# A long convolution that feeds a grouped mixture of experts: where the side work of rounds two and three stands in their first stages

## The chip, the cores and the metric

The kernel runs on one core of a Trainium2 chip. The metric is the device time of one execution in microseconds (us). Five engines work side by side, each through its own instructions in order: TensorE (PE; its weight loads are shown as PEld), VectorE (DVE), ScalarE (ACT), GpSimd (POOL) and SyncE (SP), which here only issues DMAs.

## What is computed

The reference first convolves, for 8 batches, a sequence of 5056 rows and 128 channels with a filter h, by a Fourier transform of twice the length, a product and the inverse. The 40448 rows that come out then go through 16 experts in 4 groups, each row to the best expert of its best group.

```python
Xf = np.fft.rfft(x, n=2 * S, axis=1);  Hf = np.fft.rfft(h, n=2 * S, axis=0)
x = np.fft.irfft(Xf * Hf[None], n=2 * S, axis=1)[:, :S].reshape(B * S, D)
g_idx = argmax(x @ w_group);  e_idx = argmax(xg @ w_expert[g])
out[tok] = g_w * e_w * (np.maximum(xg @ w1[g, e], 0.0) @ w2[g, e])
```

## The kernel before, in words

**Rounds and stages.** The transform is done in two factors, in three rounds of three slots each: round one (`r = 0`) takes the filter and two batches, rounds two and three (`r = 1`, `r = 2`) three batches each. A round has a first stage (`stage1`), then the groups (`groups`: the second factor, the product with the filter's transform and its inverse), which write to DRAM (`zd`). What is left of a round, its side work (`side`), is done in pieces between the steps of what follows: that of round one during round two, that of round two during round three, that of round three during the experts' blocks.

**The first stage.** It has 48 loads of 160 KB and 96 steps `k`, two for each load. Of every five loads three are folded (small matmuls, line 421, then a copy on ScalarE to `odd`, line 438, and a sum and a difference on VectorE, lines 439 and 440) and two are not (full matmuls, line 427, then one copy on ScalarE, line 444). A load's matmuls go to a pair of PSUM banks `pp`, of which rounds two and three have three. When a load has been evacuated, ScalarE's queue issues the next ones (line 404). The input tiles are named `xt` and `xy`.

**The side work.** It is a list of steps, each with a place `t` on a line of 68.55 slots. Per eighth of a round and 8 slots there are two lumps (lines 721 and 735: the last factor, into the banks `py0` and `py1`, which ScalarE copies to `yT`, line 742), at 0 and 3; the logits matmuls (line 788, read `yT`; copied to `lT`, line 793) with four transposes of rows (line 778), at 4.7; the logits' transpose (line 798) with four more, at 6.4; the remaining row transposes, at 9.5. Some forty small steps of routing on VectorE (`gate_math`) lie between 6.5 and 12.1. Then 10 or 15 scatters stand in a list, of which `send` issues one: a cast on VectorE (line 853) and an indirect DMA on GpSimd (line 854). A lump asks for rows of its successor: `zm` (line 703) behind its first matmuls, four `zt` (line 708), and a second `zm`, all in SyncE's queue.

**The order.** `run` writes one list `main` of steps with weights, and `weave` goes through it. A step of the first stage weighs `W_S1` = 0.45, two steps of each pair of groups 2.0 each, all else nearly always 0. Each weight pays for side steps in proportion, and those are emitted right behind it:

```python
s["acc"] += w / s["len"]
while s["done"] < len(s["steps"]) and (s["sacc"] < s["acc"] * s["total"] - 1e-6 or i == s["end"] - 1):
    sw, sf, small = s["steps"][s["done"]]
    if small and room[i + 1] > 0 and i < s["end"] - 1:
        light.append(sf)
```

A small step is put off and spread over the following steps of weight 0; the others are emitted at once. In rounds two and three `send` stands behind every second step (line 1666 and after). Side work of the round before starts behind step 18 of round two's first stage, and behind step 20 of round three's; that of round one ends behind step 20 of round three's.

Of the kernel before, what the change touches and what calls it, by code (L numbers as in the profile page):

```python
# [47 lines left out]
W_S1, W_END = 0.45, 2.5  # L48
# [182 lines left out]
class Kernel:  # L231
# [1391 lines left out]
    def run(self):  # L1623
        tc = self.tc
        with ExitStack() as ctx:
            self.pools(ctx)
            with ExitStack() as c2:
# [10 lines left out]
                def add(f, w=0.0):  # L1638
                    main.append((w, f))

                def late(r):
                    return [f for p in gr[r][1][NQ // 2:] for _, f in p]

                def advance(g):
                    return lambda: next(g, None)
# [11 lines left out]
                for r in range(3):  # L1657
                    if r == 1:
                        add(self.share)
                    pre, steps = gr[r]  # L1660
                    rest = late(r - 1) if r > 0 else []
                    n = len(s1[r][1])
                    t0 = self.table_0()
                    for k, f in enumerate(s1[r][1]):
                        add(f, W_S1)
                        if r > 0 and k % 2 == 1:
                            add(self.send)
                        if r == 0:
                            add(advance(more))
                        if r == 2 and ("end", 0) in mark:  # L1670
                            add(advance(t0))
                        if k >= 1:
                            for g in rest[RP * k - RP:RP * k]:
                                add(g)
                        if k == SIDE0 and r > 0:
                            add(side[r - 1][0])
                        if k == max(SIDE0 + SIDEG, END0 if r == 2 else 0) and r > 0:
                            mark["start", r - 1] = len(main)
                            if r == 2:
                                mark["end", 0] = len(main)  # L1680
                        if k >= n - PRE and (k - n) % 5 == 0:
                            add(advance(pre))
                    if r > 0:
                        add(lambda: None, W_END)
                    for p in range(0, NQ, 2):
                        for w, f in steps[p // 2]:
                            add(f, w)
                        if p >= NQ - LOAD1:
                            add(advance(s1[r + 1][0] if r < 2 else early))
# [74 lines left out]
```

## Time and profile before

| | us |
|---|---|
| median of three runs | 1758.63 |
| the three runs | 1750.66, 1758.63, 1761.71 |
| the profiled execution | 1759.51 |
| its span, first to last instruction | 1757.7 |

The profile is of one execution on one core. A stage's stretch is given in us from the span's start. Clock figures are TensorE's granted clock as a share of full speed, which is 2.4 GHz; the lower level is 1.2 GHz. "issue" is time in which an engine waited for nothing that the profile shows. TensorE runs a float32 matmul in several passes, so it shows more records than the program has matmuls: 32 for a folded load, 8 for one that is not.

### The profile page before, as it was taken

The page shows a single profiled execution, that of the slowest core. Times are in us where ns is not written, and L with a number is a line of the kernel's source. Part 1 is how long each engine was busy: PE and PEld are TensorE (multiplying, and loading weights), DVE is VectorE, ACT ScalarE, POOL GpSimd, SP SyncE. Part 2 cuts the span into 40 slices and gives each one's busy share as a digit, 9 for nine tenths or more (in the row PEclk, how much of TensorE's full clock was granted, in tenths as well). Part 3 has the DMA queues.
Part 4 walks back from the last instruction along what each step waited for, and adds up shares of the span by engine and source line. Part 5 has one row for each costly group of instructions (what it writes and reads, how often), then busy time and mean ns, then how long its engine had stood idle before and what let it go on. Part 6 is the DMA issues. An engine that isn't in the chain of part 4 may idle for free. (4 is left out here: it accounts for less than half of the span.)

```text
span 1757.7 us, 48202 instructions
## 1 busy us (share of the span) xinstructions
PE 1661.5 (95%) x16765; PEld 1299.0 (74%) x16765; DVE 1297.0 (74%) x3080; ACT 1043.0 (59%) x2461; POOL 769.0 (44%) x742
## 2 busy tenths in 40 slices
PE   8998899988898998999999999999999999999997
PEld 8677756567655556777777778787788877888987
DVE  6554598864586787777777778887787778877876
ACT  5564444443343445666666666676666666666765
POOL 1451243442454454144455545254565554334444
PEclk9999999999998999999999999999999999999999
DMA  7796677876487777555665654447545584444554
GB/s 219 229 299 204 179 249 237 275 230 182 145 247 232 244 226 212 168 165 163 171 175 167 171 152 147 133 144 227 186 148 156 166 254 136 130 129 146 156 164 152
DMA packets 281640, 330.26 MB, mean 188 GB/s; under 512 B 33335, under 2 KB 216000, under 8 KB 281368
## 3 DMA queue, kind: packets, MB, share of 16 engines
q1 hardware_dynamic: 252504, 271.00, 52.2%
q0 software_dynamic: 20608, 41.79, 6.9%
q10 hardware_dynamic: 8256, 14.10, 2.8%
q8 instruction: 140, 2.29, 0.6%
q14 instruction: 132, 1.08, 0.2%
HBM read 230.41 MB, written 96.86 MB: 186 GB/s over the span
## 5 line engine op out<-in xcount | busy, mean ns | idle before, releaser
L854 POOL DMA_INDIRECT srt<-rw,pos x320 | 344.9, 1078 | 450.0 <-DVE pos L853 173.4
L1421 POOL DMA_INDIRECT out<-orow,at x176 | 182.2, 1035 | 254.4 <-ACT at L1419 200.8
L539 DVE TENSOR_TENSOR y<-pp,hg 128x768 f32<-128x768 f32 (+1 forms) x120 | 103.8, 865 | 79.1 <-ACT hg L529 31.1
L1421 POOL DMA_INDIRECT out<-orow,sids x92 | 94.0, 1022 | 116.8 <-DVE orow L1388 83.7
L589 PE MATMUL pp<-y,cg 64*64 64x384 f32 (+1 forms) x1472 | 118.7, 444 | 14.4 <-DVE m L539 10.6
L599 ACT COPY zs<-pp 128x768 f32<-128x768 f32 (+1 forms) x118 | 85.2, 722 | 79.2 <-PE pp L589 40.2
L439 DVE TENSOR_TENSOR st<-pp,odd 128x320 f32<-128x320 f32 x90 | 44.2, 491 | 104.3 <-ACT odd L438 102.4
L521 PE MATMUL pp<-st,cg 64*64 64x192 f32 (+1 forms) x1556 | 117.8, 407 | 0.8 <-issue 0.4
L721 PE MATMUL py<-ig,zm 126*64 126x79 f32 x2048 | 95.5, 243 | 18.7 <-issue 15.1
L721 PEld LDWEIGHTS py<-ig,zm 126*64 126x64 f32 x2048 | 82.1, 142 | 39.2 <-issue 28.0
L1356 DVE SCALAR_TENSOR_TENSOR h0l<-px,h0h 128x512 fp32r<-128x512 f32 (+1 forms) x109 | 73.5, 675 | 50.1 <-ACT h0h L1355 34.9
L742 ACT COPY yT<-py 128x474 f32<-128x474 f32 (+1 forms) x96 | 44.6, 513 | 106.2 <-PE py L735 86.6
L1355 ACT ACTIVATE h0h<-px 128x512 fp32r<-128x512 f32 (+1 forms) x109 | 63.9, 586 | 73.6 <-PE px L1352 47.3
L539 DVE TENSOR_TENSOR m<-pp,hg 128x768 f32<-128x768 f32 (+1 forms) x120 | 102.9, 858 | 1.2 <-ACT hg L531 1.2
L1356 DVE SCALAR_TENSOR_TENSOR h2l<-px,h2h 128x512 fp32r<-128x512 f32 (+1 forms) x112 | 75.5, 674 | 37.8 <-ACT h2h L1355 28.9
L589 PEld LDWEIGHTS pp<-y,cg 64*64 64x64 f32 x1472 | 59.2, 133 | 53.4 <-issue 26.7
L1356 DVE SCALAR_TENSOR_TENSOR h3l<-px,h3h 128x512 fp32r<-128x512 f32 (+1 forms) x111 | 74.6, 672 | 30.2 <-ACT h3h L1355 26.8
L521 PEld LDWEIGHTS pp<-st,cg 64*64 64x64 f32 x1556 | 62.9, 134 | 40.3 <-issue 33.6
L1355 ACT ACTIVATE h3h<-px 128x512 fp32r<-128x512 f32 (+1 forms) x111 | 65.2, 587 | 37.3 <-PE px L1352 27.1
L573 POOL TENSOR_TENSOR y<-y,m 128x512 f32<-128x512 f32 x40 | 51.0, 1276 | 74.5 <-DVE m L561 42.0
L1356 DVE SCALAR_TENSOR_TENSOR h1l<-px,h1h 128x512 fp32r<-128x512 f32 (+1 forms) x111 | 74.7, 673 | 8.3 <-issue 2.9
L1355 ACT ACTIVATE h1h<-px 128x512 fp32r<-128x512 f32 (+1 forms) x111 | 65.1, 587 | 22.1 <-PE px L1352 10.0
(476 smaller groups left out, 5187.4 us busy)
## 6 DMA issues: line engine op xcount, KB each, us to landing
wr<-in_moe_w SPq DMA_DIRECT2D x373, 256.0 KB
zd<-zs SPq DMA_DIRECT2D x78, 384.0 KB
zm<-zd SPq DMA_DIRECT2D x64, 378.0 KB
cg<-in_c_g SPq DMA_DIRECT2D x102, 224.0 KB
xr<-srt SPq DMA_DIRECT2D x71, 260.0 KB
hg<-hd SPq DMA_DIRECT2D x80, 128.0 KB
zd<-zs SPq DMA_DIRECT2D x39, 256.0 KB
xt<-in_x ACTq DMA_DIRECT2D x54, 160.0 KB
```

Of the source, the lines that this page charges most:

```text
L439: nc.vector.tensor_tensor(out=all_st[:, 0:2 * HALF, d], in0=even, in1=odd, op=ALU.add)
L521: nc.tensor.matmul(px[c * 64:c * 64 + 64, b, to], lhsT=k, rhs=data[:, of], start=begin, stop=i == len(steps) - 1 or p == 0 and i == 1, til ...
L539: nc.vector.tensor_tensor(out=t[:, :, 0:w].rearrange("p t (r u d) -> p t r u d", r=2, u=nu), in0=taken(px, part).unsqueeze(1).broadcast_to ...
L573: (nc.gpsimd if r == 0 else nc.vector).tensor_tensor(out=y[:, :, 0:w], in0=y[:, :, 0:w], in1=m[:, :, 0:w], op=ALU.add)
L589: nc.tensor.matmul(pz[c][h:h + 64, 0:w], lhsT=wt[c * 64:c * 64 + 64, k + h:k + h + 64], rhs=y[c * 64:c * 64 + 64, part, 0:w], start=part = ...
L599: nc.scalar.copy(out=z[:, 0:n, 0:w], in_=pp[:, 0:n, 0:w])
L721: nc.tensor.matmul(pys[q][c:c + 64, col(n, u)], lhsT=zms[q][:, n % QB, k:k + 64], rhs=self.ig[:, 0:NH], start=n % QB == 0 and u == 0, stop ...
L742: nc.scalar.copy(out=self.yT[:, k:k + QB * c1], in_=pys.pop(q)[:, 0:QB * c1])
L854: ins = self.nc.gpsimd.indirect_dma_start(out=self.srt, out_offset=bass.IndirectOffsetOnAxis(ap=k["pos"][0:p, j:j + 1], axis=0), in_=k["rw ...
L1355: nc.scalar.activation(out=hh, in_=p, func=AF.Relu)
L1356: nc.vector.scalar_tensor_tensor(out=hl, in0=p, scalar=0.0, in1=hh.bitcast(F32), op0=ALU.max, op1=ALU.subtract)
L1421: ins = self.nc.gpsimd.indirect_dma_start(out=self.a["out"], out_offset=bass.IndirectOffsetOnAxis(ap=ids, axis=0), in_=o, in_offset=None, ...
```

## The change

The weight of a first-stage step in rounds two and three is no longer 0.45: it is 4.5 for each tenth step (`k % 10 == 9`, the second step of the last of five loads, which follows two that are not folded) and 0 for all others. Round one keeps 0.45.

```diff
                     for k, f in enumerate(s1[r][1]):
-                        add(f, W_S1)
+                        add(f, 10 * W_S1 if r > 0 and k % 10 == 9 else 0.0 if r > 0 else W_S1)
                         if r > 0 and k % 2 == 1:
                             add(self.send)
```

So lumps, logits and row transposes stand only behind those steps, and the small steps, put off, are spread over the nine that follow. GpSimd's instructions stand in the same order as before.

TensorE in round three's first stage, from the second half of a lump that stands inside a folded load up to the next logits matmuls (line 788). `py` are the lump's banks, `xy` and `xt` input tiles. Before:

```order
L735 MATMUL py_7273<-igt,zt 64x2x79 x2
L735 MATMUL py_7293<-igt,zt 64x2x79 x2
L421 MATMUL pp<-f,xy 64x80 x8
L421 MATMUL pp<-f,xt_83 64x80 x16
L427 MATMUL pp<-f,xy 128x158 x4
L427 MATMUL pp<-f,xt_84 128x158 x2
L788 MATMUL py_7386<-yT,wge 32x512 x4
L778 MATMUL py_7394<-ident,yT 128x128 x4
L427 MATMUL pp<-f,xt_84 128x158 x2
```

The same lump and logits now:

```order
L427 MATMUL pp<-f,xy 128x158 x4
L427 MATMUL pp<-f,xt_84 128x158 x4
L721 MATMUL py_7323<-ig,zm 64x79 x12
L721 MATMUL py_7343<-ig,zm 64x79 x12
L735 MATMUL py_7323<-igt,zt 64x2x79 x2
L735 MATMUL py_7343<-igt,zt 64x2x79 x2
L735 MATMUL py_7323<-igt,zt 64x2x79 x2
L735 MATMUL py_7343<-igt,zt 64x2x79 x2
L735 MATMUL py_7323<-igt,zt 64x2x79 x2
L735 MATMUL py_7343<-igt,zt 64x2x79 x2
L788 MATMUL py_7372<-yT,wge 32x512 x4
L778 MATMUL py_7380<-ident,yT 128x128 x4
```

The lump has moved behind two loads that are not folded, and no load stands any more between it and the logits matmuls.

TensorE at the end of round two's first stage; line 971 is a routing matmul of the side work, line 521 the groups' first. Before, with the rest of the lump (six rows of line 735) and the routing behind these:

```order
L421 MATMUL pp<-f,xt_80 64x80 x8
L778 MATMUL py_3664<-ident,yT 128x128 x2
L421 MATMUL pp<-f,xt_80 64x80 x8
L421 MATMUL pp<-f,xy 64x80 x16
L421 MATMUL pp<-f,xt_81 64x80 x16
L721 MATMUL py_3724<-ig,zm 64x79 x8
L721 MATMUL py_3740<-ig,zm 64x79 x8
```

Now, with this lump and the last row transposes ahead of these:

```order
L421 MATMUL pp<-f,xt_80 64x80 x16
L421 MATMUL pp<-f,xy 64x80 x16
L971 LDWEIGHTS ltri
L971 MATMUL pp<-tot,ltri 128x16
L972 LDWEIGHTS ltri
L972 MATMUL pp<-spare_326,ltri 128x16
L971 LDWEIGHTS ones
L971 MATMUL pp<-tot,ones 128x16
L972 LDWEIGHTS ones
L972 MATMUL pp<-spare_326,ones 128x16
L421 MATMUL pp<-f,xt_81 64x80 x16
L521 MATMUL pp<-st,first 64x192
```

The lump stood behind the last load and now stands ahead of the last three; the last load is followed by line 521.

## Rows read from the trace of the kernel before

**Rows 1.** The page: the span, and busy time, share of the span and instructions of each engine.

```profile
span 1757.7 us, 48202 instructions
PE 1661.5 (95%) x16765; PEld 1299.0 (74%) x16765; DVE 1297.0 (74%) x3080; ACT 1043.0 (59%) x2461; POOL 769.0 (44%) x742
```

**Rows 2.** Busy time by stretch: the stretch and its length, busy us (records) of PE, PEld, DVE, ACT and POOL, granted clock, DMA share and GB/s. The first stages of rounds one, two and three.

```profile
4.00:49.00 45.00, 42.25 (x1104) 39.34 (x1104) 27.31 (x84) 25.51 (x50) 3.71 (x12) 1.00 0.74 215
...
137.00:212.60 75.60, 65.42 (x1466) 56.79 (x1466) 36.34 (x126) 34.43 (x77) 15.06 (x19) 0.95 0.63 188
...
368.40:472.50 104.10, 84.08 (x1642) 69.97 (x1641) 50.02 (x213) 41.26 (x95) 35.91 (x40) 0.92 0.65 186
```

**Rows 3.** TensorE's waits in round three's first stage (368.4 to 472.5 us): who waited for what, us in total, times, longest.

```profile
PE pp L421 <- issue: 6.5, 14, 1.1
PE py L721 <- issue: 4.1, 7, 1.2
PE pp L421 <- ACT st L444: 2.5, 3, 1.4
PE pp L427 <- ACT odd L438: 2.1, 2, 1.3
PE pp L589 <- issue: 1.3, 1, 1.3
PE pp L427 <- issue: 1.1, 1, 1.1
PE py L721 <- DMA zm<-zd: 0.5, 1, 0.5
```

**Rows 4.** The same for round two's first stage (137 to 212.6 us).

```profile
PE pp L421 <- issue: 3.5, 8, 1.1
PE pp L427 <- DMA zt<-zd: 2.9, 1, 2.9
PE pp L427 <- ACT odd L438: 1.1, 1, 1.1
PE pp L421 <- ACT odd L438: 1.0, 1, 1.0
```

**Rows 5.** TensorE in order of time in round three's first stage: start, us, what, records. An unfolded load, a folded load, a lump, and parts of the next lump.

```profile
417.27 1.24 PE L427 MATMUL pp<-f,xy 128*128 128x158 f32 x8
418.44 0.78 PE L421 MATMUL pp<-f,xt 64*64 64x80 f32 x32
419.15 1.86 PE L721 MATMUL py<-ig,zm 126*64 126x79 f32 x48
420.94 1.04 PE L735 MATMUL py<-igt,zt 64*64 64x158 f32 x24
...
429.14 1.04 PE L721 MATMUL py<-ig,zm 126*64 126x79 f32 x24 [0.46 <-DMA zm<-zd]
```

**Rows 6.** ScalarE by line: busy us, mean ns of one, idle before. The first three of round three's first stage, the last of round two's.

```profile
L438 ACT COPY odd<-pp 128x320 f32<-128x320 f32 x30 | 12.4, 431 | 25.1 <-remote 14.7 <-PE pp L421 3.6 <-DVE posf L985 2.5
L444 ACT COPY st<-pp 128x632 f32<-128x632 f32 x18 | 11.9, 689 | 8.5 <-issue 2.3 <-DMA xt<-in_x 1.9 <-DMA zm<-zd 1.8
L742 ACT COPY yT<-py 128x474 f32<-128x474 f32 x12 | 6.2, 557 | 15.5 <-PE py L735 8.8 <-PE pp L972 2.4 <-PE pp L421 2.3
...
L742 ACT COPY yT<-py 128x316 f32<-128x316 f32 x11 | 4.2, 425 | 10.0 <-PE py L735 7.3 <-DMA zt<-zd 2.7
```

**Rows 7.** VectorE by line in round three's first stage, the two parts of a folded load's evacuation.

```profile
L439 DVE TENSOR_TENSOR st<-pp,odd 128x320 f32<-128x320 f32 x30 | 14.6, 488 | 50.4 <-ACT odd L438 48.6 <-ACT pos L853 1.7
L440 DVE TENSOR_TENSOR st<-pp,odd 128x312 f32<-128x312 f32 x30 | 14.2, 472 | 0.0
```

**Rows 8.** TensorE in order of time at the end of the two first stages: round three's, from its last folded load to the groups, then round two's.

```profile
468.61 0.71 PE L421 MATMUL pp<-f,xt 64*64 64x80 f32 x24 [0.20 <-issue]
469.24 1.06 PE L788 MATMUL py<-yT,wge 128*32 128x512 f32 x8
...
472.52 0.37 PE L521 MATMUL pp<-st,first 64*64 64x192 f32 x1 [1.62 <-DVE st L439]
...
209.80 0.77 PE L421 MATMUL pp<-f,xt 64*64 64x80 f32 x29
210.50 1.31 PE L721 MATMUL py<-ig,zm 126*64 126x79 f32 x32
...
212.63 0.37 PE L521 MATMUL pp<-st,first 64*64 64x192 f32 x1
```

**Rows 9.** SyncE's queue in order of time: the loads that the lump at 419.15 us asks for behind its first `zm`.

```profile
420.64 2.37 SPq L708 DMA_DIRECT2D zt<-zd  x4
423.11 0.36 SPq L703 DMA_DIRECT2D zm<-zd  x1
```

**Rows 10.** TensorE in order of time through a folded load and a lump of round three's first stage; then the first and the last of five scatters on GpSimd.

```profile
446.04 0.78 PE L421 MATMUL pp<-f,xy 64*64 64x80 f32 x32
446.76 0.35 PE L721 MATMUL py<-ig,zm 126*64 126x79 f32 x2
...
454.12 1.86 PE L735 MATMUL py<-igt,zt 64*64 64x158 f32 x24
...
443.96 0.97 POOL L854 DMA_INDIRECT srt<-rw,pos  x1 [3.68 <-DVE pos L853]
...
449.09 0.99 POOL L854 DMA_INDIRECT srt<-rw,pos  x1 [0.30 <-issue]
```

## The prediction

> **What bounds the kernel now.** I read the page's totals first, then busy time by stage, then TensorE's waits inside the two stages that the change touches, then the durations, and last the places where time is lost.
>
> TensorE is busy 95% of a span of 1757.7 us [rows 1]. The change acts only in two stretches of that: round two's first stage, 137 to 212.6 us, and round three's, 368.4 to 472.5 us, together 179.7 us. There TensorE is busy 65.42 of 75.60 and 84.08 of 104.10 us, VectorE 36.34 and 50.02, ScalarE 34.43 and 41.26 [rows 2]. So TensorE is the bound there too, with 10.2 and 20.0 us idle, and the granted clock averages 0.95 and 0.92 of full speed. Time at the lower level costs the missing share: 0.05 of 75.6 is 3.8 us, 0.08 of 104.1 is 8.3 us. All idle and lost clock together is 42 us, 2.4% of the kernel; that is about the most that any order of these stages could give back.
>
> What is TensorE waiting for? In round three [rows 3] 13.0 us (6.5 + 4.1 + 1.3 + 1.1) are "issue", where no semaphore of the profile held it, and only 4.6 us (2.5 + 2.1) are for ScalarE to free a bank pair that a load was evacuated from. In round two [rows 4] it is 3.5 us issue and 2.1 us ScalarE. The 2.9 us for a DMA there stand behind the first lump of side work, which keeps its place, and stay.
>
> The work of one cycle of five loads at full speed: a folded load takes TensorE 0.78 us, an unfolded one 1.24 us, so 3 x 0.78 + 2 x 1.24 = 4.8 us; a lump of side work in round three takes 1.86 + 1.04 = 2.9 us [rows 5]. ScalarE needs 0.431 us for a folded load and 0.689 for an unfolded one [rows 6], 2.7 us a cycle; VectorE 0.488 + 0.472 = 0.96 us for a folded one [rows 7], 2.9 us a cycle. In the three folded loads VectorE (0.96) is slower than TensorE (0.78), and in the two unfolded ones it has nothing to do for the loads. That is the imbalance the order could use.
>
> **The change part by part.** No instruction is added or removed; the sums of weights shift slightly. In round two the first stage's weight behind the start of the side work goes from 77 x 0.45 = 34.65 to 8 x 4.5 = 36 of about 127, so all six lumps stay in or at the end of the stage. In round three it goes from 75 x 0.45 = 33.75 to 7 x 4.5 = 31.5 of about 115: one logits step with its transposes leaves the first stage for the groups. It costs TensorE the same there, so I count nothing.
>
> (a) Steps that depend on each other now stand back to back. One weight of 4.5 is worth 2.4 slots in round two and 2.7 in round three, more than the 1.7 between a second lump and the logits step. The order shows the logits matmuls (line 788) right behind a lump's last matmul, once in round two and twice in round three. They read yT, which ScalarE must first copy out of two banks: 2 x 0.557 us in round three, 2 x 0.425 in round two [rows 6]. Before, other loads' matmuls filled that time. ScalarE is free by then: its 0.689 us for the last unfolded load fits under the lump's 2.9. Price: 2 x 1.11 + 0.85 = 3.1 us. Bounds 2.5 (the two copies overlap a little) and 6 (another copy of 0.689 us and the issue of loads stand ahead each time).
>
> (b) The ends of the stages. The groups' first matmul (line 521) waits for the last folded load to be evacuated. In round three 3.2 us passed between that load's end (468.61 + 0.71) and 472.52; the logits step and transposes covered part and 1.62 us were idle. In round two a lump stood there and nothing was idle: its 2.1 us (209.80 + 0.77 to 212.6) were enough [rows 8]. Now round three gets a lump of 2.9 us there, and its wait falls to about 0.3: 1.3 us saved. Round two has the lump moved ahead of the last three loads, and no side matmul stands between the last load and the groups. The chain alone is 0.431 + 0.488 + 0.472 = 1.4 us, the measured one up to 3.2; I take the 2.1 of the same place. Sum +0.8 us, bounds -0.3 and +2.
>
> (c) Lumps one cycle apart. A lump's second pair of zm rows is asked for only when four zt loads have been issued (420.64 to 423.01, then 423.11), and that one was in use not before 429.14, after a wait of 0.46 us, 10.0 us behind the lump's start at 419.15 [rows 5, 9]. The closest lumps of round three are now 2.9 + 4.8 = 7.7 us apart at full speed, and the second half comes 0.9 us later, 8.6: a wait of 1.4 us, at one place. In round two the loads are two thirds of the size and no lump waited for zm [rows 4]; I take nothing there. +1.4 us; bounds 0 and 5 (both stages, each close pair).
>
> (d) What the change frees. The 6.7 us of waits for ScalarE [rows 3, 4] come where copies of side work stand between a load's matmuls and its own evacuation. Now they stand only ahead of the first folded load. There they still delay it: 1.1 us for a lump, against three bank pairs, that is 3 x 0.78 = 2.3 us of matmuls, that TensorE may run ahead; then the slower VectorE must catch up. I take half, -3.4 us; bounds 0 and -6.7.
>
> (e) The issue gaps. In round three a folded load and a lump took from 446.04 to 455.98 (454.12 + 1.86), 9.9 us, where the durations above make 0.78 + 2.9 = 3.7; the matmuls came in ones and twos while GpSimd ran scatters one behind the other from 443.96 to 450.08 [rows 10]. So 6.2 us went at one place, half-rate clock included. Round one's first stage, without scatters, has 1104 matmul records in 45 us, more per us than the later ones, at clock 1.00 and 42.25 us busy [rows 2]; dense matmuls alone don't do it. The change leaves the scatters in their order: in the program VectorE prepares 10 in round two's first stage before and after, and 29 and 26 in round three's. What changes is only which matmuls meet them. I take 0, with bounds of -8 (one place like the one shown goes, and a little more) and +12 (two more).
>
> The Trainium skill, page "Runtime: NRT & Kernel Launch", section "Instruction fetch mechanics", says that an engine's sequencer fetches the next block of instructions over its own DMA queue while it executes the present one, so that this is mostly hidden. If so, packing dense matmuls together can't lengthen such a gap, (e) is 0 for sure, and the sum stands as it is. The 13.0 us of issue in round three speak against "hidden" if the gaps are of that kind, which no row here shows; by the trace the bound of +12 stays.
>
> Sum: 3.1 + 0.8 + 1.4 - 3.4 + 0 = +1.9 us. The profiled execution took 1759.5 us, 1.8 more than its span and 0.9 above the median of 1758.63; on it that is 1761.4, on the median 1760.5. I predict 1760.5 us. Its own range, from the bounds with not all at one end, is 1750 to 1775.
>
> **The rivals.** Faster: the scatters meet the sparse unfolded loads more often, and the dense stretches come when GpSimd is done. For it: the loss is large, 13.0 + 8.3 us in round three and 3.5 + 3.8 in round two, 28.6 us, and the new order gives TensorE a fixed sparse stretch of 2.5 us in each cycle. Against it: scatters go out one per load, so they run through whole cycles. If two thirds go, 19 us, the time is 1741. Chance 0.10.
>
> Slower: the lump now always stands directly ahead of three folded loads, so the densest instructions stand in one piece of 2.9 + 2.3 us, and under running scatters each such piece stalls as at 446 us [rows 10]. Price 6.2 us apiece; some five lumps of both stages stand under scatters. It decides from three more stalls than now: 18.6 us, 1779. For it: before, unfolded loads or single folded ones often separated the dense pieces. Against it: total instructions and scatters are the same, and the stall shown came with a single folded load ahead of the lump. Chance 0.14.
>
> A third, without a change of sign that could be told: the waits for ScalarE don't fall at all, (d) is 0, and the time is 1764. It lies inside the forecast's case.
>
> **How the numbers follow.** A difference of 1%, 17.6 us, is about what a measurement of this kernel can tell from no change. The forecast, within it, has 0.76; the faster rival 0.10; the slower one 0.14. The range reaches into both rivals to 1744 and 1778.
>
> **What would show it.** Right: in the changed profile, ScalarE's copies of yT (line 742) hold up line 788 for about a microsecond at three places; line 521 waits some 2 us for VectorE at the start of round two's groups and hardly at round three's; line 721 waits for zm once or twice; waits of lines 421 and 427 for ScalarE are near half of 6.7 us; both first stages together last 178 to 186 us. Wrong: if the issue gaps or the lower clock of these stages change by more than 10 us either way, step (e) fails; if the stages keep their length and the total moves by more than 1%, I missed a consequence in the groups or in the experts' blocks.

## The result, and the profile after

On the same chip, side by side, the changed kernel took 1769.54 us (median of 7 runs, 1767.52 to 1776.69) and the kernel before 1755.38 (median of 7): a ratio of 1.0082, 95% interval 1.0061 to 1.0104. It is slower by 14.2 us. Three further groups of runs were each made on a chip of their own, called B, C and D; the chip of this result is called A. (Its number is not on record. By the time of the kernel before, 1755.38 and 1753.95 us, A could be C; it is neither B nor D.) On B the ratio was 1.0041 [1.0025, 1.0057], on D 1.0047 [1.0024, 1.0070]; on C the changed kernel was not run.

The profiled execution of the changed kernel took 1776.69 us, 17.2 more than that of before; it is the slowest of its runs, so its differences are about 3 us too large in all. First its page's totals, the answer to [rows 1]:

```profile
span 1775.0 us, 48183 instructions
PE 1670.5 (94%) x16765; PEld 1303.7 (73%) x16765; DVE 1294.4 (73%) x3081; ACT 1047.0 (59%) x2460; POOL 769.7 (43%) x742
```

Then busy time by stretch (columns as in [rows 2]): round two's first stage and groups, round three's first stage and groups.

```profile
139.00:222.60 83.60, 67.54 (x1467) 57.49 (x1467) 35.76 (x128) 35.81 (x82) 15.43 (x19) 0.94 0.61 184
222.60:377.20 154.60, 145.55 (x2204) 85.86 (x2208) 135.71 (x318) 70.61 (x190) 55.75 (x52) 0.99 0.76 244
377.20:486.90 109.70, 82.98 (x1632) 68.83 (x1628) 48.39 (x208) 38.69 (x85) 34.24 (x38) 0.91 0.58 164
486.90:676.70 189.80, 177.03 (x2456) 111.43 (x2447) 140.90 (x343) 79.88 (x215) 96.00 (x87) 0.96 0.75 233
```

Against before the first stages are longer by 83.6 - 75.6 = 8.0 and 109.7 - 104.1 = 5.6 us [rows 2], together 13.6 of the 17.3 us of the spans. Round two's groups, 155.8 us before, lost 1.2; round three's, 186.1 before, gained 3.7; round one gave 2.0 more, and the experts 0.8 less. (Round one's order is the same in both kernels, so two executions can differ by some 2 us there without a cause in the change.) In the first stages TensorE is busy 1.0 us longer in sum, and 12.6 us longer idle. So the question is what it waits for. In round three's first stage (view as in [rows 3]):

```profile
PE pp L427 <- ACT odd L438: 8.8, 6, 5.2
PE pp L421 <- issue: 4.8, 9, 1.1
PE py L788 <- ACT yT L742: 4.4, 2, 3.7
PE py L721 <- issue: 2.0, 4, 1.1
PE py L735 <- issue: 1.8, 3, 0.8
PE pp L427 <- issue: 1.4, 2, 1.0
```

In round two's (as in [rows 4]):

```profile
PE pp L427 <- DVE st L440: 3.6, 1, 3.6
PE pp L421 <- issue: 3.0, 8, 0.5
PE py L798 <- ACT lT L793: 1.8, 1, 1.8
PE pp L427 <- ACT odd L438: 1.8, 4, 0.4
PE pp L421 <- ACT odd L438: 1.7, 2, 0.8
...
PE pp L521 <- DVE st L439: 1.1, 1, 1.1
...
PE py L788 <- ACT yT L742: 0.5, 1, 0.5
PE py L778 <- ACT yT L742: 0.5, 1, 0.5
```

The 3.6 us there are the place that showed 2.9 us for `zt` before. Issue fell from 13.0 us to 10.5 in round three (4.8 + 2.0 + 1.8 + 1.4, and 0.5 of line 589) and from 3.5 to 3.2 in round two. What rose are the waits for copies: of a bank pair (lines 421 and 427 for `odd`) from 4.2 us in both stages to 12.3, of which one wait alone is 5.2, and of `yT` and `lT`, hardly there before, to 7.2, of which one is 3.7. (The 2.5 us that line 421 waited for `st` before are gone; with them the bank pairs' waits were 6.7.)

**One cycle, read closely.** TensorE in the changed kernel's round two, in order of time: a logits step, its transposes, three folded loads, and the first unfolded one.

```profile
166.29 1.16 PE L788 MATMUL py<-yT,wge 128*32 128x384 f32 x8 [0.51 <-ACT yT L742]
167.39 0.66 PE L778 MATMUL py<-ident,yT 128*128 128x128 f32 x4
167.97 0.78 PE L421 MATMUL pp<-f,xy 64*64 64x80 f32 x32
168.58 0.73 PE L421 MATMUL pp<-f,xt 64*64 64x80 f32 x32
169.13 0.73 PE L421 MATMUL pp<-f,xy 64*64 64x80 f32 x32
170.31 1.31 PE L427 MATMUL pp<-f,xt 128*128 128x158 f32 x8 [0.45 <-ACT odd L438]
```

VectorE beside it, the evacuation of the first of these folded loads:

```profile
169.33 0.49 DVE L439 TENSOR_TENSOR st<-pp,odd 128x320 f32<-128x320 f32 x1 [9.24 <-ACT odd L438]
169.74 0.47 DVE L440 TENSOR_TENSOR st<-pp,odd 128x312 f32<-128x312 f32 x1
```

ScalarE, its copy for the same load:

```profile
168.87 0.43 ACT L438 COPY odd<-pp 128x320 f32<-128x320 f32 x1 [0.20 <-PE pp L421]
```

Three folded loads fill the three bank pairs in 1.9 us (167.97 to 169.86). The first pair is free when VectorE's line 440 ends, at 169.74 + 0.47 = 170.21, and line 427 starts at 170.31. The view names ScalarE's `odd`, but that was done at 169.30; VectorE came last. The first folded load was done at 168.75; its evacuation took 1.46 us from there, the two folded loads behind it 1.1, and TensorE stands still for the rest. This comes again at 175.72, 183.55 and 200.15 with 0.44 or 0.45 us. Two waits of 0.83 us, at 190.39 and 220.71, are longer because the routing matmuls (line 971) take one of the pairs between the loads.

### The profile page after: what moved, and what is told of

It is laid out like the page before. It is cut to its first block, busy times and chain, and to the rows that moved or that the text cites. A ratio compares the mean times of both kernels' runs of the same rounds, so it can differ in the third digit from the quotient of the medians.

```text
span 1775.0 us, 48183 instructions
## 1 busy us (share of the span) xinstructions
PE 1670.5 (94%) x16765; PEld 1303.7 (73%) x16765; DVE 1294.4 (73%) x3081; ACT 1047.0 (59%) x2460; POOL 769.7 (43%) x742
## 5 line engine op out<-in xcount | busy, mean ns | idle before, releaser
L1421 POOL DMA_INDIRECT out<-orow,sids x92 | 94.0, 1022 | 118.2 <-DVE orow L1388 83.6
L721 PE MATMUL py<-ig,zm 126*64 126x79 f32 x2048 | 91.5, 241 | 9.5 <-issue 8.8
```

Of the source, the lines that this page charges most:

```text
L721: nc.tensor.matmul(pys[q][c:c + 64, col(n, u)], lhsT=zms[q][:, n % QB, k:k + 64], rhs=self.ig[:, 0:NH], start=n % QB == 0 and u == 0, stop ...
L1421: ins = self.nc.gpsimd.indirect_dma_start(out=self.a["out"], out_offset=bass.IndirectOffsetOnAxis(ap=ids, axis=0), in_=o, in_offset=None, ...
```

## The experiments

The theories: "packing" (all side work at one place of a cycle leaves the bank pairs and the copies of `yT` and `lT` without cover) and its parts; that one held load issue makes the loss; and that scatters and issue gaps do.

**The changed kernel on another chip, and a held issue (chip B; before there 1685.62 us).** In the changed kernel of chip A line 427 waited once for 5.2 us, where other cycles show 0.4 to 1.2. ScalarE's queue around it (`ACTq` are its DMA issues), then SyncE's:

```profile
446.56 0.32 ACTq L404 DMA_DIRECT2D xt<-in_x  x1
446.92 0.22 ACT L955 CAST tot<-cs 128x16 bf16<-128x16 f32 x1 [5.98 <-DMA first<-in_c_g]
```

```profile
444.50 0.24 SPq L1089 DMA_DIRECT2D tabr<-tabd  x1
```

ScalarE did nothing from 440.95 until the load at 446.56 was issued. In the program that load waits for the completion of the table's read `tabr` (line 1089), eight DMAs before it in the rotation of completion semaphores, and that read went out only at 444.50.

> The changed kernel once more, beside the kernel before on the same chip, as the base for the other three. Both theories expect the ratio measured before, 1.008 (14 us). Its two first stages should again be near 84 and 110 us, and ScalarE should again stand still for about 5 us in round three's, until the load of an input tile is issued behind the read of a small table.

1692.53 us (12 runs), 6.9 slower than before. The loss is there on a chip that runs the whole kernel 4% faster, but half as large as expected. The two first stages lasted 76.1 and 87.4 us, not 84 and 110, and the longest wait for `odd` was 2.5 us, not 5.2.

```diff
-        for _ in range(4 if self.tp() is self.cp else 7):
+        for _ in range(7 if self.tp() is self.cp else 7):
```

The table's read moves so that no load waits for it.

> The changed kernel, with the read of round three's small table three steps later in SyncE's queue. In the program the issue of an input load on ScalarE's queue waits for the DMA that used the same one of eight completion semaphores before it; in the changed kernel that is this table read, in the kernel before it is not. With the read three steps later no load on ScalarE's queue waits for it. Theory 'held issue' (ScalarE, and TensorE behind it, is held by a DMA issue that waits for an unrelated DMA): round three's first stage loses the gap of 5.2 us and the whole is 4 to 6 us faster than the changed kernel, about 1.005 of the kernel before. Theory 'packing' (the cost is dependent steps standing back to back and three folded loads in a row): no change, 1.008.

1691.58 us, 1.0041 [1.0022, 1.0060]. In round three's first stage the waits for `odd` fell from 6.3 us (longest 2.5) beside it to 3.8 (longest 1.2), but issue rose from 1.4 to 3.2, and the stage lasted 86.9 us instead of 87.4. The held issue is real. On this chip, where it cost 2.5 us at one place, taking it away changed the time by 0.95 us, less than these runs can tell, and the loss stayed. On chip A, where it cost 5.2 us, it was not tried; at the same place TensorE waited 4.7 us in the run with round three alone, below, and 4.3 in the repeat on chip D.

**One round alone (chip B).**

```diff
-add(f, 10 * W_S1 if r > 0 and k % 10 == 9 else 0.0 if r > 0 else W_S1)
+add(f, W_S1 if r != 1 else 10 * W_S1 if k % 10 == 9 else 0.0)
```

> The change in round two's first stage alone; round three's keeps its weights of 0.45. 'Packing' expects the loss there in full: that stage near 83.6 us instead of 75.6, +6 to +8 us in all. 'Held issue' expects only what the loads' issues happen to wait for in this order: between 0 and +8, with round three's stage as in the kernel before (104 us).

1689.56 us, 1.0026 [1.0011, 1.0041].

```diff
+add(f, W_S1 if r != 2 else 10 * W_S1 if k % 10 == 9 else 0.0)
```

> The change in round three's first stage alone. In the program a load's issue waits for the table read here too. 'Held issue' expects at least 5 us of loss, with the gap of some 5 us in that stage; 'packing' expects +5 to +8 us (stage near 110 us) spread over waits of TensorE for ScalarE of 0.4 to 1.3 us each and for yT. Both together, with the round-two run: the two losses add up to about 14 us.

1687.79 us, 1.0014 [0.9999, 1.0029]. The two losses, 3.9 and 2.2 us, add up to 6.1 of the whole change's 6.9, though the second by itself can't be told from none. Both are less than "packing" expected (6 to 8 and 5 to 8). Round two's first stage packed (first kernel), then in the old order (second), columns as above:

```profile
137.31:211.76 74.45, 62.26 (x1467) 53.93 (x1467) 35.77 (x128) 35.57 (x82) 15.40 (x19) 0.98 0.67 199
```

```profile
136.33:205.51 69.18, 60.49 (x1466) 52.84 (x1466) 36.60 (x126) 33.82 (x77) 15.21 (x19) 1.00 0.69 205
```

The packed one is 5.3 us longer. Idle time accounts for 3.5 of these (12.2 against 8.7), a granted clock of 0.98 in place of 1.00 for most of the rest. Its waits that the other lacks are 3.6 us for `odd`, 2.2 for `yT` and `lT` and 1.1 at line 521, partly in place of issue (1.2 for 2.7). Round three's is 89.1 us packed and 88.5 not, though one logits step with its transposes (1.06 + 0.66 us of matmuls in [rows 8]) has left it.

**The parts of the packing (chip C; before there 1753.95 us).** Three other sets of places: behind the third folded load; behind each unfolded one; behind the third folded and the second unfolded one. The changed kernel was not run on this chip and the kernel before was not profiled on it, so these three are compared with the time of the kernel before and with one another.

```diff
+add(f, W_S1 if r == 0 else 10 * W_S1 if k % 10 == 5 else 0.0)
```

> The changed kernel with the side work of rounds two and three only behind the third folded load (k % 10 == 5), so just ahead of the unfolded loads and no longer ahead of three folded ones; a cycle has one place for it, as in the changed kernel, and steps that depend on each other still stand back to back. Theory 'banks' (three folded loads in a row behind a lump, whose bank pairs ScalarE and VectorE free later than TensorE wants them): the waits of lines 421 and 427 for ScalarE's odd copy fall from 4.6 us in round two's stage (first chip 3.7) to under 2, round two's stage is 2 to 4 us shorter than with the lumps ahead of the folded loads (75 to 76 us on the second chip, 83.6 on the first), and the kernel is 3 to 6 us faster than the changed one, 0 to 4 us slower than the kernel before. Rival 'dependent steps' (the copies of yT and lT between adjacent side steps are what costs): the stage stays within 1 us of the changed kernel's, with the waits for yT and lT as there. Rival 'nothing but the number of places' (any order that gathers side work at one place costs the same): the same time as the changed kernel, with the waits moved elsewhere.

1762.21 us, 1.0045 [1.0026, 1.0064]. Its waits in round two's stage:

```profile
PE pp L421 <- issue: 2.8, 8, 0.4
PE py L798 <- ACT lT L793: 2.6, 1, 2.6
PE pp L421 <- DMA xt<-in_x: 1.8, 3, 0.9
PE py L721 <- DMA zm<-zd: 1.8, 1, 1.8
PE pp L421 <- ACT st L444: 1.7, 2, 0.8
```

Not one wait for `odd` is left, as "banks" says, but those for `lT` and `yT` stay (3.6 us, with two of 0.5), others come (`zm`, `st`), and the stage lasted 79.5 us. In round three 0.6 us are left for `odd` and 6.6 for `yT`. It is 8.3 us slower than the kernel before, where "banks" named 0 to 4. The changed kernel lost 14.2 us on A and 6.9 on B and D, so whether easing the banks alone gained anything on C can't be told.

```diff
+add(f, W_S1 if r == 0 else 5 * W_S1 if k % 10 in (7, 9) else 0.0)
```

> The changed kernel with two places in a cycle of five loads instead of one, behind the first and behind the second unfolded load (5 * W_S1 at k % 10 in (7, 9)): a load stands between a lump and the logits step that reads its yT, and the three folded loads still stand in a row. Theory 'dependent steps': the waits for yT and lT (2.1 us in round two's stage on the second chip, 5 us in round three's on the first) fall under 0.5 us and the kernel gains 2 to 5 us on the changed one. Theory 'banks': the waits for ScalarE's odd copy stay at 4 to 5 us in round two's stage and round two's stage stays over 73 us; the kernel gains at most 2 us. Where both hold: 2 to 3 us gained, the rest stays.

1761.31 us, 1.0036 [1.0020, 1.0052]. The mirror image in its waits: none for `yT` or `lT` in either stage, and 3.1 and 5.1 us for `odd`. A loss of 7.4 us stays, but its place is another. Round two's first stage, then round three's and its groups, as above:

```profile
137.71:213.19 75.48, 65.04 (x1462) 56.91 (x1466) 36.31 (x126) 33.97 (x76) 15.49 (x19) 0.94 0.64 190
370.04:472.38 102.34, 82.43 (x1634) 67.17 (x1630) 49.61 (x210) 38.40 (x85) 36.01 (x40) 0.93 0.61 177
472.38:664.50 192.12, 178.08 (x2454) 113.80 (x2445) 140.71 (x341) 79.07 (x215) 93.94 (x86) 0.96 0.72 230
```

The two first stages lasted 177.8 us together, 15.3 less than in the run before this one (79.5 + 113.7).

```diff
+add(f, W_S1 if r == 0 else 5 * W_S1 if k % 10 in (5, 9) else 0.0)
```

> The changed kernel with two places in a cycle of five loads, behind the third folded and behind the second unfolded load (5 * W_S1 at k % 10 in (5, 9)). Both parts of the cost are halved if both theories hold: lumps ahead of three folded loads at about every second place, dependent steps parted by two or three loads. I expect round two's stage at 70 to 73 us on the second chip (69.2 in the order before, 75 to 76 in the changed order), the waits for yT and lT under 0.5 us, and a time within 3 us of the kernel before. If it is slower than the kernel before by as much as the changed kernel (7 us), neither adjacency nor the place ahead of the folded loads is the cause, and something that the trace does not show (the weights moving work between stages) is.

1751.20 us, 0.9981 [0.9965, 0.9997]. With both parts eased the loss is gone: 0.8 and 0.6 us for `odd`, none for `yT` or `lT` in round two, 3.3 in round three. Round two's stage lasted 76.5 us, above the 70 to 73 that I expected from chip B. The same three stretches:

```profile
137.04:213.51 76.47, 66.26 (x1466) 57.22 (x1466) 35.63 (x126) 34.43 (x77) 15.37 (x19) 0.93 0.61 186
367.16:468.12 100.96, 84.96 (x1646) 69.89 (x1638) 50.39 (x214) 40.23 (x88) 35.10 (x40) 0.90 0.65 189
468.12:652.90 184.78, 169.02 (x2435) 104.08 (x2434) 140.37 (x336) 78.14 (x214) 94.27 (x86) 0.97 0.74 233
```

The two first stages lasted 177.4 us, no less than the 177.8 of the run above. Of the 10.7 us between the two profiled spans 7.3 lie in round three's groups and 3.2 in round two's (156.85 and 153.65 us); a logits step that has left round three's first stage in the run above accounts for 1.7 of that. So by the medians the loss goes only when both parts are eased; by the first stages, parting the dependent steps alone had done as much, and the loss of the run above may be that of the moved step. Round three's groups are longer in the two kernels of A and C where it moved (189.8 and 192.1 us) than in the three where it stayed (186.1, 181.9 and 184.8). That was not tried on C; the last run below tries it on D.

**Scatters (chip C).** In the kernel before, `send` no longer stands between the loads:

```diff
-                        if r > 0 and k % 2 == 1:
+                        if False:
```

> The kernel before, with no scatter given out between the loads of rounds two's and three's first stages (the lines that send one per two steps there are off, so the scatters go out later, among the groups and the experts; nothing of the computation is left out). Theory 'scatters make the issue gaps': the waits of TensorE put down to issue in round three's first stage (13.0 us on the first chip, 1.9 on the second) fall under 1 us, and that stage is shorter by about as much; the total may be longer, since the experts' gathers then wait for later scatters. Rival 'dense matmuls make them': the issue waits stay as in the kernel before on the same chip.

One run: 1789.46 us, 35.5 above the median of before. Issue waits in round three's first stage were 5.8 us (4.2 + 1.3 + 0.3), against 13.6, 10.8 and 8.6 in the three kernels above on this chip (the kernel before has no profile there): fewer, but far from under 1. The list of scatters was still emptied there, in two trains, 413.6 to 419.7 and 446.4 to 458.9 us, and 3.8 of the 4.5 us in the loads lie inside them or within 1 us of the end. That issue gaps and scatters go together is supported; which causes which was not settled. Most of the 35 us went to the groups, 166.7 and 207.7 us long (155.8 and 186.1 in the kernel before on chip A), where TensorE waited once 10.8 and once 12.2 us for ScalarE.

**Side by side on one chip (chip D; before there 1690.85 us).**

> The changed kernel once more, unchanged, as the yardstick of this group on one chip. It was 14.2 us (0.8%) and 6.9 us (0.4%) slower than the kernel before on two chips; I expect 6 to 15 us here, and round two's first stage at 5 us or more over the kernel before's.

1697.74 us, 1.0047 [1.0024, 1.0070].

> The kernel with two places per cycle, behind the third folded and behind the second unfolded load (5 * W_S1 at k % 10 in (5, 9)), a second time, beside the changed kernel. 'Adjacency' (side work split over two places two or three loads apart costs nothing, whereas gathered at one place, or at two places one load apart, it costs 0.4 to 0.8%): within 4 us of the kernel before, and 6 to 15 us faster than the changed kernel. 'Luck of a chip' (it was 2.8 us faster than the kernel before in one call): over 5 us slower than the kernel before here.

1685.26 us, 0.9972 [0.9956, 0.9988]: 12.5 us faster than the changed kernel on the same chip, and for the second time faster than the kernel before. The two first stages of the changed kernel there, then of the one with two places:

```profile
137.74:216.04 78.30, 63.49 (x1467) 54.93 (x1467) 36.10 (x128) 35.49 (x82) 15.41 (x19) 0.96 0.64 192
365.76:455.10 89.34, 72.72 (x1633) 62.47 (x1629) 48.56 (x208) 38.57 (x85) 32.37 (x37) 0.96 0.71 199
```

```profile
138.55:206.44 67.89, 60.86 (x1467) 53.51 (x1467) 35.52 (x126) 34.17 (x77) 15.27 (x19) 0.97 0.70 208
355.54:441.21 85.67, 73.36 (x1645) 62.11 (x1638) 50.49 (x214) 40.12 (x88) 34.96 (x40) 0.96 0.77 218
```

They are 10.4 and 3.7 us shorter, 14.1 in sum, which covers the 12.5 us of the medians. (The profiled spans differ by 8.4 only: in this pair the experts' blocks took 1087.6 us with two places and 1080.0 without.) The waits for `odd`, `yT` and `lT` were 18.3 us in the two stages of the first and 0.5 in those of the second, where line 427 also waited 2.9 us for VectorE's part (line 440). The same lump and logits step as in the close reading, with two places; TensorE, then VectorE's last row for the first folded load:

```profile
160.82 1.78 PE L721 MATMUL py<-ig,zm 126*64 126x79 f32 x32
162.54 0.77 PE L735 MATMUL py<-igt,zt 64*64 64x158 f32 x16
163.12 0.73 PE L421 MATMUL pp<-f,xy 64*64 64x80 f32 x32
163.68 0.73 PE L421 MATMUL pp<-f,xt 64*64 64x80 f32 x32
164.23 0.73 PE L421 MATMUL pp<-f,xy 64*64 64x80 f32 x32
164.89 0.85 PE L788 MATMUL py<-yT,wge 128*32 128x384 f32 x8
165.68 0.66 PE L778 MATMUL py<-ident,yT 128*128 128x128 f32 x4
166.17 1.24 PE L427 MATMUL pp<-f,xt 128*128 128x158 f32 x8
```

```profile
164.85 0.47 DVE L440 TENSOR_TENSOR st<-pp,odd 128x312 f32<-128x312 f32 x1
```

Nothing waits here. The logits step stands where TensorE would have had no bank pair: VectorE frees the first at 165.32, line 427 wants one at 166.17. And while the folded loads run, ScalarE has copied the `yT` that the logits read. One displacement pays twice.

```diff
+add(f, W_S1 if r == 0 else 3.4 * W_S1 if k % 10 in (5, 7, 9) else 0.0)
```

> Three places per cycle, behind the third folded and behind both unfolded loads (3.4 * W_S1 at k % 10 in (5, 7, 9)). 'Adjacency': dependent steps are parted by a load or more and a lump stands ahead of three folded loads at two of eight places in each stage, so waits for yT, lT are under 1 us and those for ScalarE's odd copy about 1 to 2 us in round two's stage; the time is within 4 us of the two places just named. If the number of places itself matters (the more evenly the side work lies, the better), it is 2 us or more faster than two places.

1687.63 us, 0.9984 [0.9963, 1.0006]: not told apart from two places, so nothing here shows that the number of places matters by itself. `odd` cost 2.7 and 3.1 us in its stages, and `lT` and `yT` 2.6 in round three, all more than expected; the time does not follow these waits one for one.

```diff
+add(f, W_S1 if r == 0 else 10 * W_S1 if k % 10 == 9 and r == 1 else 10.8 * W_S1 if k % 10 == 9 else 0.0)
```

> The changed kernel with 10.8 in place of 10 * W_S1 in round three alone, so that the logits step with its transposes that the change pushes out of round three's first stage (from 33.75 to 31.5 of weight) stays in it, at its end; the packing is as in the changed kernel. Theory 'the moved step costs nothing, the packing costs it all': within 2 us of the changed kernel on the same chip; round three's stage 2 to 3 us longer, its groups as much shorter. Rival 'the moved step costs in the groups' (the groups grew by 3.7 us on the first chip, of which its own matmuls are 1.7, and by 6 us with two places one load apart, where it moved too; they shrank by 1 to 4 us where it stayed): 3 to 5 us faster than the changed kernel.

1705.17 us, 1.0095 [1.0070, 1.0120], and both theories missed: it is 7.4 us slower than the changed kernel. Round three's first stage lasted 94.1 us instead of 89.3, and its groups 160.3 instead of 160.4, though TensorE was busy 2.6 us longer in the one and 2.5 us shorter in the other. So on this chip the step's place does not show in the length of the groups; that it made the 3.7 us of chip A or the 7.3 of chip C is neither shown nor excluded by that. How much of the 4.7 us in the first stage is its price can't be told from one execution: round two's first stage, where this kernel and the changed one have the same code, lasted 78.3 us there and 73.9 here:

```profile
136.91:210.81 73.90, 61.07 (x1466) 52.56 (x1466) 35.49 (x126) 35.35 (x82) 15.42 (x19) 1.00 0.69 202
```

The same caution holds for the 10.4 us by which two places shortened that stage. Where the rest of the 7.4 us is stays open: the profiled execution was the fastest of six, and its span is only 1.6 us over the other's.

## Why the prediction was right, and where it was wrong

The forecast of no change that a measurement of 1% could tell held, and 1769.54 lies in the range from 1744 to 1778. That is owed to the width of the range and not to the sum: the loss is clear at 0.8%, 14.2 us, and the sum had +1.9 for it. That 1769.54 is only 9.0 us over the 1760.5 named is in part luck, since the kernel before came out 3.2 us lower in the comparison than in the three runs that I started from. By the terms, on the profile of chip A:

- (a) Dependent steps: right as a mechanism, with the wrong sizes. Predicted were three waits of line 788 for `yT`, 3.1 us with a bound of 6. They came at the three places, and two cost 0.65 and 0.5 us, less than the 1.11 and 0.85 that I had priced; the third cost 3.7. With 0.5 us for line 778, and 1.8 for `lT`, which I had left out, it is 7.2 us. The large one, with ScalarE's row beside it:

```profile
420.41 1.01 ACT L742 COPY yT<-py 128x474 f32<-128x474 f32 x2 [4.35 <-remote]
```

  The banks were written by 417.27, and ScalarE stood idle until 420.41, while scatters ran until 419.53. ScalarE had nothing to do, as I had said, and still did not copy. What held it ("remote") no row says. The kernel before has four such stretches in this stage, 14.7 us together, all ahead of copies to `odd` [rows 6]. That one now comes through because it falls on a copy without cover is likely and not shown.
- (b) Ends of the stages: round three's wait of 1.62 us [rows 8] went, as predicted; round two got one of 1.1 us where I had 2.1. Net -0.5 instead of +0.8, inside its bounds.
- (c) Waits for `zm`: none in either stage; 1.4 us too many, and its lower bound was right. "Once or twice" at line 721 failed.
- (d) The step that failed most. I took half of 6.7 us as saved; the waits of lines 421 and 427 for ScalarE's evacuations became 12.3 us, so the term is +5.6 instead of -3.4, outside its bounds of 0 and -6.7. Two things are in that. The held issue is 5.2 us at one place, and I had no term for it. The rest is 7.1 us against 6.7: nothing was saved. There I had reckoned with 0.78 us for a folded load, the length of its row, so that three bank pairs let TensorE run 2.3 us ahead. But the rows overlap: in the close reading folded loads start 0.61 and 0.55 us apart, and three take 1.9 us. The chain of 1.4 us that I used in (b) fits under two loads of 0.78; it does not fit under the 1.1 us that the two folded loads behind the first one take. So the first unfolded load behind three folded ones in a row waits 0.44 us or more, unless a side step stands among or behind them. Before, one often did, as the lump at 419.15 us [rows 5]; the change took it away. That the order puts VectorE's slow part together was in my paragraph on the work of one cycle, as an imbalance "the order could use".
- (e) Issue gaps: 16.5 us before, 13.7 after, -2.8 of -8 to +12. Against that stands the granted clock, 0.94 and 0.91 for 0.95 and 0.92 [rows 2]; at 1% of 83.6 and of 109.7 us that is about 2 us of loss. The rival "slower" had the right sign and the wrong cause: it wanted longer issue gaps, and they got shorter. The rule that I quoted from the Trainium skill, page "Runtime: NRT & Kernel Launch", section "Instruction fetch mechanics", that fetching is mostly hidden, is neither shown nor refuted by this: packing did not lengthen the gaps, and no row says what they are. The profile's DMA view has no instruction packet that starts between 203 and 208.3 us of the changed kernel, so the gaps from 204.8 to 208.2 us ended without one.

With the measured terms the sum is 7.2 - 0.5 + 0 + 5.6 - 2.8 + 2 = 11.5 us, of 13.6 in the two stages, which lasted 193.3 us together where I had named 178 to 186. Two single waits, of 5.2 and 3.7 us, make up 8.9 of it. On chips B and D the loss is half. ScalarE's long stall at `yT` is missing there (1.3 us in place of 4.4), and the held issue is 2.5 and 4.3 us; but on D `lT` cost 3.6 us in place of 1.8. Which of these halves the loss is not shown.

## What to carry to other kernels

Where loads come in a short cycle of unlike kinds, look for the place in it where the evacuation falls behind, and put independent work right there: the same logits step cost a wait of 0.45 us ahead of the folded loads and none behind them. Reckon that place with the distance of starts in a dense row, not with the length of a row. Steps that depend on each other through another engine want a load between them. On chip D both together made the kernel 12.5 us faster than the changed one; what each is worth alone these runs don't show. A wait that is short now because something stands before it is a cost to the change that takes that something away, so ask of each gap not only what it costs but what fills it.

## What the hardware showed that I had not expected

- The same kernel took 1755.38, 1685.62, 1753.95 and 1690.85 us in four groups of runs, on three chips or four. In round three's first stage in the old order issue waits were 13.0 us on chip A and 1.9 on chip B. A difference of 0.4% between two kernels is only seen on one chip.
- Issue gaps come as a trickle: in the changed kernel's round two, 204.8 to 208.2 us, TensorE did four matmul records or one, then nothing for 0.25 to 0.51 us, five times, in a folded load whose row otherwise is 0.78 us long.
- A DMA issue in ScalarE's queue can hold that engine's computing: 5.6 us, from 440.95 to 446.56, for a transfer of another queue.
